# Streaming heads moved around the second layer in a two-layer decode kernel, with double loads for them and two norm stages in one step

## The chip, the cores and the metric

The kernel runs on one core of one Trainium2 chip. The metric is the device time of one execution in microseconds (us); lower is better. The core has a tensor engine (PE; its weight loads are listed apart as PEld), a vector engine (DVE), a scalar engine (ACT), GpSimd (POOL) and SyncE (SP), which here issues nearly all DMA transfers. Sixteen DMA engines move the data from HBM to the on-chip memory (SBUF).

## The reference

Eight sequences decode one token each. A layer is grouped-query attention over a cache, followed by a small dense network, each behind a layer norm and with a residual. Two such layers run one after the other, with the same weights and the same caches:

```python
# x: 8 x 1 x 512; k_cache, v_cache: 8 batches x 8 kv heads x 8192 keys x 128, bf16
# wq: 512 x 4096, wo: 4096 x 512 (32 query heads, 4 to a kv head); w1: 512 x 1792, w2: 1792 x 512
def _A_ref(x, k_cache, v_cache, wq, wo):
    q = (x @ wq) as 32 heads
    k = jnp.repeat(k_cache, rep, axis=1); v = jnp.repeat(v_cache, rep, axis=1)
    scores = jnp.einsum("bhqd,bhkd->bhqk", q, k) * (Dh ** -0.5)
    p = _softmax(scores, axis=-1)
    return jnp.einsum("bhqk,bhkd->bhqd", p, v) as rows @ wo
def _B_ref(x, w1, w2):
    return _silu(x @ w1) @ w2

x = x + _A_ref(_layernorm(x), A_k_cache, A_v_cache, A_wq, A_wo)
x = x + _B_ref(_layernorm(x), B_w1, B_w2)
x = x + _A_ref(_layernorm(x), A_k_cache, A_v_cache, A_wq, A_wo)
x = x + _B_ref(_layernorm(x), B_w1, B_w2)
```

Each cache has 134 MB in all. Both layers read all of it, so what the first layer leaves in SBUF need not be loaded again for the second.

## The kernel before

**Tasks, steps and pieces.** A task is one kv head of one batch in one layer: `(layer, b, g)`. There are 128. A task has four steps, and a step `c` handles one piece of 2,048 keys (K, 0.5 MB) and one piece of V (0.5 MB). For a K piece PE transposes it in two halves into PSUM (`emit_t`, L545), ACT copies the first half back (L554) and DVE the second (L556), and PE makes the scores (`emit_s`, L579). The softmax of a task runs in the steps after it: maximum on DVE (L590, L592) with a POOL reduction over partitions (L594), exponential on ACT (L603) after L599 and L601, sum (L609, L611), transposes of the probabilities (`emit_pt`, L619). V is used six steps (`LAG`) after K (`emit_pv`, L639).

**The arena.** The pieces live in an arena of 28 slots of 0.5 MB. Five of the eight heads of a batch (heads 3 to 7) are *kept*: the transposed K pieces of the first layer, 20 slots, stay until the second layer has used them (one of them is parked in PSUM for a while), and three V pieces of the last head too. The other three heads (0 to 2) are *streaming*: each layer loads them anew.

**The order of tasks.** `make_tasks` writes the order. For each batch `b` it puts the kept heads of the first layer (five tasks), then a block of streaming tasks, then the second layer of the kept heads (five tasks), and then the kept heads of the next batch. The block has five streaming tasks, six for the first and the last batch. They are the second layer of streaming heads of earlier batches (`behind`) and the first layer of streaming heads of later ones (`ahead`). No streaming task stands between the second layer of a batch and the kept heads of the next. Three streaming tasks end the order.

**The loads.** `plan_loads` and `lay_loads` go through all K and V pieces in the order of need, in half steps, and give each the slot that comes free first; `after` is the half step that frees it. A load may be a *double*: two neighbouring pieces of a head, 1 MB in one DMA into two neighbouring slots, with rows of 8 KB. The kernel before allows doubles for kept heads and for the last batch's second layer, where both slots come free at least 8 half steps (`WIDE`) ahead of need. SyncE issues the loads in the order of this list (`issue_until`), each as soon as its slot is free, and all on one queue: a load whose slot is still in use holds those behind it.

**The chain between the layers.** When the last kept head of a batch is done (`last0`, six steps after its K), its row goes on to the second layer through a chain of small jobs: the rest of the output projection, a layer norm, the dense network, another layer norm, and the queries of the second layer. The jobs stand in a list, and each step of the tasks takes at most one of each kind in the step's own order: `MID` in its middle, `TILE` ahead of its scores on PE, `TURN` at its end. A layer norm has four stages: `n[0]` sums on DVE and POOL (L661, L663), `n[1]` centres and sums squares (L669, L689, L690 on DVE, L692 on POOL), `n[2]` reads POOL's sum and makes a first guess at the root (L708, L710, L698, L703), and `n[3]` makes a second and scales the row (L698, L703, L717). The engines take their instructions in the order written, so on DVE the stages stand between the copies L556 and the maximum L590.

Of the kernel before, what the change touches and what calls it, by code (L numbers as in the profile page):

```python
# [17 lines left out]
KEEP = 20  # L18
KEEPV = 3
PARK = 1  # L20
LAG = 6
WIDE = 8
AHEAD = 8
# [114 lines left out]
def make_tasks(nb, nkv, keep_from):  # L138


    first = int(keep_from)
    a = [[(0, b, g) for g in range(first)] for b in range(nb)]
    kept = [[(0, b, g) for g in range(first, nkv)] for b in range(nb)]
    c = [[(1, b, g) for g in range(first, nkv)] for b in range(nb)]
    d = [[(1, b, g) for g in range(first)] for b in range(nb)]
    ahead = [t for b in range(1, nb) for t in a[b]]
    behind = []
    tasks = a[0] + kept[0]
    na = 0
    for b in range(nb):  # L150
        if b:
            tasks += kept[b]
        size = -(-(2 * first * (nb - 1)) // nb) if b in (0, nb - 1) else 2 * first * (nb - 1) // nb
        must = max(0, first * min(b + 1, nb - 1) - na)
        nd = size if b == nb - 1 else min(len(behind), first, size - must)
        tasks += behind[:nd]
        del behind[:nd]
        take = ahead[na:na + size - nd]
        na += len(take)
        tasks += take  # L160
        if b + 1 == nb:
            tasks += behind
        tasks += c[b]
        behind += d[b]
    tasks += d[nb - 1]
    assert na == len(ahead)
    return tasks


def rows_of(d, kept):  # L170
    return 0 if (d.g, d.k) in kept else d.layer, d.b, d.g, d.k // 2
# [22 lines left out]
def lay_loads(tasks, kept, parked, keptv, nslot, ngran, single):  # L194

    at = {t: i for i, t in enumerate(tasks)}
    wanted = []
    late = closing_from(tasks, kept)
    for i, (layer, b, g) in enumerate(tasks):
        for k in range(ngran):  # L200
            c = i * SPT + k
            if layer == 0 or (g, k) not in kept:
                last = i if layer or (g, k) not in kept - parked else at[(1, b, g)]
                wanted.append(Load("K", layer, b, g, k, -1 if c < AHEAD else 2 * (c - LEAD if c >= late else c), 2 * (last * SPT + k) + 1))
            elif (g, k) in parked:
                wanted.append(Load("C", layer, b, g, k, 2 * (c - 1), 2 * c + 1))
            if layer == 0 or (g, k) not in keptv:
                last = i if layer or (g, k) not in keptv else at[(1, b, g)]
                wanted.append(Load("V", layer, b, g, k, 2 * (c + LAG), 2 * (last * SPT + k + LAG)))
    wanted.sort(key=lambda d: (d.need, d.kind))  # L210
    free = [-2] * nslot
    loads, copies = [], []
    while wanted:
        d = wanted.pop(0)
        if d.kind == "C":
            d.slot = max((j for j in range(nslot) if free[j] < d.need - 1), key=lambda j: (free[j], j))
            free[d.slot] = d.free
            copies.append(d)
            continue
        mate = None  # L220
        if d.k % 2 == 0 and ((d.g, d.k) in kept or d.layer and d.b == tasks[-1][1]) and rows_of(d, kept) not in single:
            same = [e for e in wanted if (e.kind, e.layer, e.b, e.g, e.k) == (d.kind, d.layer, d.b, d.g, d.k + 1)]
            mate = same[0] if same else None
            s = min(range(nslot - 1), key=lambda j: (max(free[j], free[j + 1]), j))
            after = max(free[s], free[s + 1])
            if after > d.need - WIDE or d.need < 0 or len(wanted) == 1:
                mate = None
        if mate:
            wanted.remove(mate)
# [27 lines left out]
def _build(ctx, nc, A_x, A_k_cache, A_v_cache, A_wq, A_wo, B_w1, B_w2, out):  # L257
    B, _sq, D = A_x.shape
# [3 lines left out]
    REP = HQ // HKV  # L262
    KT = D // 128
# [168 lines left out]
    with nc.Block() as block:  # L432

        @block.sync
        def _(sync_eng):
# [346 lines left out]
                )  # L782

            TILE, MID, TURN = range(3)

            def chain_of(b):
                x0, x1, x2 = [XT[n][:, :, b:b + 1] for n in range(3)]
                xn = one[2]
                qt2, rq2 = QT2[b % 2], f"QT2_{b % 2}"

                def attended():
                    sum_rows(x1, "XT1", x0, "XT0", 1.0)

                def up():
                    tiles([(t, xn[:, k, :], across(w1_sb[:, k, :], 0, FT)[:, t], k == 0, k == KT - 1)
                           for k in range(KT) for t in range(NT)], ["w1", "xn1"])

                hv = MISC[:, 0:FT * QR:QR]

                def expo():  # L800
                    upright(FT)
                    op(act, lambda: act.activation(eh, hv, ACT.Tanh, scale=0.5), reads=["MISC"], writes=["eh"])

                def silu():
                    op(dve, lambda: dve.scalar_tensor_tensor(hsT, eh, 1.0, hv, op0=ALU.add, op1=ALU.mult),
                       reads=["MISC", "eh"], writes=["hsT"])

                def down(q0, q1):
                    def run():
                        tiles([(t, hsT[:, q:q + 1], across(w2_sb[:, q, :], 0, KT)[:, t], q == 0, q == FT - 1)  # L810
                               for q in range(q0, q1) for t in range(NT)], all_of("w2") + ["hsT"])
                    return run

                AC = KB // QR

                def ask(a, k0, k1):
                    def run():
                        tiles([(t, xn[:, k, :], across(wq_sb[:, k, :], a * AC, (a + 1) * AC)[:, t],
                                k == 0, k == KT - 1) for k in range(k0, k1) for t in range(NT)], ["wq", "xn1"])
                    return run  # L820

                def answer(a):
                    def run():
                        upright(AC)
                        op(dve, lambda: dve.tensor_copy(qt2[:, a * AC:(a + 1) * AC], MISC[:, 0:KB:QR]),
                           reads=["MISC"], writes=[rq2])
                    return run

                n1, n2 = ln_stages(x1, "XT1", 1, one), ln_stages(x2, "XT2", 1, one)

                def gained():
                    sum_rows(x2, "XT2", x1, "XT1", 0.5)
                    n2[0]()

                def met():
                    attended()
                    n1[0]()

                return (
                    [(TURN, met), (MID, n1[1]), (MID, n1[2]), (TURN, n1[3])]  # L840
                    + [(TILE, up), (MID, expo), (TURN, silu), (TILE, down(0, FT // 2)), (TILE, down(FT // 2, FT))]
                    + [(TURN, gained), (MID, n2[1]), (MID, n2[2]), (TURN, n2[3])]
                    + [x for a in range(HQ // AC)
                       for x in ((TILE, ask(a, 0, KT // 2)), (TILE, ask(a, KT // 2, KT)), (TURN, answer(a)))]
                )

            def closing(n):
# [94 lines left out]
            emit_q(0)  # L942

            chain = []
            chain_b = [None]
            turn = [0]
            last0 = {b: max(task_at[(0, b, g)] for g in range(HKV)) for b in range(B)}
            first1 = {b: min(task_at[(1, b, g)] for g in range(HKV)) * SPT for b in range(B)}
# [19 lines left out]
            for c in range(NC + LAG):  # L968
                if c < NC:
                    layer, b, g, k = where(c)  # L970
                if c and c % SPT == 0 and c < NC:
                    assert layer == 0 or not chain or chain_b[0] != b
                    emit_q(c // SPT)
                ready = c < NC and (c < AHEAD or layer == 1 and (g, k) in kept)
                if ready:
# [24 lines left out]
                if c >= LAG and (c - LAG) % SPT == SPT - 1:  # L1000
                    tj = (c - LAG) // SPT
                    layer, b, g = tasks[tj]
                    if layer == 0:
                        heads[b].append(g)
                    elif b == B - 1:
                        heads[B].append(g)
                    if layer == 0 and tj == last0[b]:
                        assert not chain and turn[0] == b
                        chain.extend([(TILE, lambda b=b: add_rest(b))] + chain_of(b))
                        chain_b[0] = b  # L1010
                        turn[0] = b + 1
            assert not queue and not chain

# [38 lines left out]
```

## Time and profile before

| | |
|---|---|
| median of 3 runs | 1145.84 us (1143.29 to 1145.88) |
| the profiled execution | 1136.29 us |
| its span, first to last instruction | 1134.5 us |
| mean granted PE clock | 0.926 of full speed |
| PE busy | 935.0 us, 82% |
| DVE, ACT, POOL busy | 49%, 43%, 10% |
| HBM read | 452.47 MB |
| time of SyncE's queue on the 16 DMA engines | 99.1% of the span |

The page divides the span into 40 slices; the DMA row gives the mean busy share of the 16 DMA engines in tenths, and the row below it the GB/s that they moved. A stretch of time can be asked for by itself; its line gives the stretch, its length, the busy time of PE, PEld, DVE, ACT and POOL with the number of instructions, the granted PE clock, the DMA share and the GB/s. A timeline line gives the start, the length, engine, source line, operation, what is written and read, and in brackets the idle time before it and what ended it.

### The profile page before, as it was taken

The numbers are of one execution on the slowest core, as the hardware profiler recorded it, in microseconds if no ns is written. First come the engines' busy times: TensorE is split into PE (matmuls) and PEld (weight loads), VectorE is DVE, ScalarE is ACT, GpSimd is POOL, SyncE is SP. The second block draws the span as 40 slices with busy tenths as digits, with TensorE's granted clock in tenths as the row PEclk, the third lists the DMA queues.
The fourth block names the chain that finished last, engine by engine and source line by source line (L and its number), as shares of the span: only waits on it lengthen the run. The fifth ranks groups of instructions, "written<-read, shape, count | busy, mean of one in ns | idle before, by whom it ended". The sixth has DMA issues, their size and how long they took to land.

```text
span 1134.5 us, 42794 instructions
## 1 busy us (share of the span) xinstructions
PE 935.0 (82%) x18792; PEld 698.9 (62%) x18792; DVE 558.3 (49%) x1710; ACT 491.0 (43%) x778; POOL 117.3 (10%) x300
## 2 busy tenths in 40 slices
PE   6687887888888888888888888888878888888796
PEld 4366664666566665666567665676566655665565
DVE  6444554445534553446444553446444553455444
ACT  5354442455335542554245542554245432554332
POOL 0000111001100101001100111001100111011010
PEclk9699998999879997999889997999789997999888
DMA  9999999999999999999999999999999999999995
GB/s 376 413 413 415 392 407 412 420 411 385 405 419 416 391 408 417 419 411 392 412 419 415 394 403 418 418 403 393 407 419 411 381 408 419 417 388 367 396 420 224
DMA packets 95550, 455.26 MB, mean 401 GB/s; under 512 B 10620, under 2 KB 10884, under 8 KB 69380
## 3 DMA queue, kind: packets, MB, share of 16 engines
q1 hardware_dynamic: 95348, 452.51, 99.1%
q8 instruction: 148, 2.42, 0.9%
q14 instruction: 38, 0.31, 0.1%
q10 hardware_dynamic: 16, 0.01, 0.0%
HBM read 452.47 MB, written 0.01 MB: 399 GB/s over the span
## 4 chain that ended last, share of the span: by engine, by line
DMA 40%; PE 37%; DVE 11%; ACT 5%; issue 5%; SPq 2%; POOL 0%; POOLq 0%; ACTq 0%; DVEq 0%
DMA arena<-in_A_v_cache_dram 32%; PE TPp L545 18%; PE SCp L579 9%; DVE arena L556 9%; DMA arena<-in_A_k_cache_dram 7%; PE OTp L639 4%; ACT arena L554 4%; PE TPp L619 2%; DMA wq<-in_A_wq_dram 2%; SPq L401 2%; PE MISC L754 2%; ACT P L603 1%; PE KEPTp L545 1%; DVE small L628 1%; DVE small L599 0%
## 5 line engine op out<-in xcount | busy, mean ns | idle before, releaser
L554 ACT COPY arena<-TPp 128x1024 bf16<-128x1024 bf16 x344 | 348.1, 1012 | 393.1 <-PE TPp L545 389.7
L545 PE MATMUL TPp<-ident,arena 128*128 128x128 bf16 x5504 | 377.8, 223 | 28.1 <-DMA arena<-in_A_k_cache_dram 22.3
L556 DVE COPY arena<-TPp 128x1024 bf16<-128x1024 bf16 x344 | 238.0, 692 | 329.7 <-PE TPp L545 327.0
L545 PEld LDWEIGHTS TPp<-ident,arena 128*128 128x128 bf16 x5504 | 317.9, 100 | 118.1 <-issue 62.1
L639 PE MATMUL OTp<-PT,arena 128*128 128x32 bf16 x8192 | 292.0, 179 | 56.6 <-DMA arena<-in_A_v_cache_dram 52.7
L639 PEld LDWEIGHTS OTp<-PT,arena 128*128 128x128 bf16 x8192 | 252.6, 97 | 136.0 <-DMA arena<-in_A_v_cache_dram 105.7
L579 PE MATMUL SCp<-arena,QB 128*32 128x512 bf16 x2048 | 223.8, 429 | 71.5 <-DVE arena L556 24.0
L603 ACT ACTIVATE P<-SCp,small 128x512 bf16<-128x512 f32 x128 | 87.9, 687 | 203.5 <-DVE small L601 157.8
L590 DVE TENSOR_REDUCE small<-SCp 128x1 f32<-128x512 f32 x128 | 88.5, 692 | 103.7 <-PE SCp L579 102.5
L579 PEld LDWEIGHTS SCp<-arena,QB 128*32 128x32 bf16 x2048 | 59.8, 96 | 112.5 <-ACT arena L554 53.4
L594 POOL PARTITION_ALL_REDUCE small<-small x128 | 47.5, 371 | 620.9 <-DVE small L592 620.9
L611 POOL PARTITION_ALL_REDUCE small<-small x128 | 55.2, 431 | 332.4 <-DVE at L653 146.5
L619 PE MATMUL TPp<-ident,P 128*128 128x128 bf16 x512 | 54.9, 235 | 26.4 <-ACT arena L554 14.6
L619 PEld LDWEIGHTS TPp<-ident,P 128*128 128x128 bf16 x512 | 31.5, 103 | 35.5 <-ACT arena L554 20.1
L623 DVE COPY PT<-TPp 128x256 bf16<-128x256 bf16 x128 | 37.3, 291 | 20.8 <-PE TPp L619 18.9
L609 DVE TENSOR_SCALAR small<-small 128x4 f32<-128x4 f32 x128 | 28.7, 224 | 37.9 <-ACT P L603 37.9
L592 DVE TENSOR_SCALAR small<-small 128x4 f32<-128x4 f32 x128 | 29.4, 229 | 4.5
L599 DVE TENSOR_TENSOR small<-small 128x4 f32<-128x4 f32 x128 | 20.0, 157 | 20.9 <-POOL small L594 20.9
L767 DVE STREAM_TRANSPOSE MISC<-MISC 128x128 f32<-128x128 f32 (+2 forms) x40 | 22.1, 552 | 10.0 <-PE MISC L754 10.0
L754 PE MATMUL MISC<-wo,at 128*32 128x128 bf16 x1024 | 26.0, 231 | 0.0
L603 ACT ACTIVATION_READ_ACCUMULATOR P<-SCp,small 128x1 f32 x128 | 24.7, 193 | 0.0
L601 DVE TENSOR_REDUCE small<-small 128x1 f32<-128x4 f32 x128 | 20.1, 157 | 4.4
(102 smaller groups left out, 329.7 us busy)
## 6 DMA issues: line engine op xcount, KB each, us to landing
arena<-in_A_v_cache_dram SPq DMA_DIRECT2D x131, 1024.0 KB, 13.8
arena<-in_A_v_cache_dram SPq DMA_DIRECT2D x226, 512.0 KB, 6.6
arena<-in_A_k_cache_dram SPq DMA_DIRECT2D x216, 512.0 KB, 7.2
arena<-in_A_k_cache_dram SPq DMA_DIRECT2D x68, 1024.0 KB, 20.1
arena<-in_A_wo_dram SPq DMA_DIRECT2D x8, 512.0 KB, 12.7
wq<-in_A_wq_dram SPq DMA_DIRECT2D x1, 4096.0 KB, 24.8
w<-in_B_w_dram SPq DMA_DIRECT2D x1, 1792.0 KB, 22.3
arena<-in_B_w_dram SPq DMA_DIRECT2D x3, 512.0 KB, 16.9
```

Source lines behind the costliest of these rows:

```text
L545: lambda c=c: pe.transpose(tpv[:, c, :], chunk(slot, h * GRP + c), ident[:, :])
L554: op(act, lambda: act.copy(dst, bank[:, :]), reads=[rt], writes=[r_half(slot, h)])
L556: op(dve, lambda: dve.tensor_copy(dst, bank[:, :]), reads=[rt], writes=[r_half(slot, h)])
L579: lambda t=t: pe.matmul(SCp[bank][t * QR:(t + 1) * QR, :], QB[qn][:, NGRAN - 1 - k:NGRAN - 1 - k + QR], keys[:, t * KB:(t + 1) * KB], star ...
L590: op(dve, lambda: dve.tensor_reduce(mxp[st][:, :], SCp[bank][:, :], AX.X, ALU.max), reads=[f"SC{bank}"], writes=[f"mxp{st}"])
L594: op(pool, lambda: pool.partition_all_reduce(mxa[st][:, :], mxr[st][:, :], 128, bass.bass_isa.ReduceOp.max), reads=[f"mxr{st}"], writes=[f ...
L603: op(act, lambda: act.activation(P[:, :], SCp[bank][:, :], ACT.Exp, bias=nb[st][:, 0:1], scale=SM_SCALE, accum_out=rs[st][:, :]), reads=[f ...
L611: op(pool, lambda: pool.partition_all_reduce(ssa[st][:, :], ssm[st][:, :], 128, bass.bass_isa.ReduceOp.add), reads=[f"ssm{st}"], writes=[f ...
L619: lambda c=c: pe.transpose(tpv[:, c, :], P[:, c * 128:(c + 1) * 128], ident[:, :])
L623: op(dve, lambda: dve.tensor_copy(PT[:, :, :, :], tpv.rearrange("p c (t q) -> p c t q", q=QR)[:, :, :, 0:NGRAN * REP]), reads=[f"TP{tb}"], ...
L639: lambda n=n, cc=cc: pe.matmul(otp, chunk(slot, n), PT[:, cc % CPB, (cc // CPB) % NT, cc // (CPB * NT)::NGRAN].unsqueeze(2).to_broadcast([ ...
L754: lambda t=t, col=col, w=w, start=start, stop=stop: pe.matmul(MISC[t * QR:(t + 1) * QR, 0:math.prod(w.shape[1:])], spread(col), w, start=s ...
```

## The change

It makes three edits.

1. `make_tasks` puts four streaming tasks (`WINDOW`) between the kept heads of a batch and its second layer. The remaining ten go behind the second layer, one or two ahead of each batch's next kept heads: 1, 1, 2, 1, 2, 1, 2 behind batches 0 to 6. In both places tasks of `behind` come first, as far as enough of `ahead` is done in time.
2. `lay_loads` allows a double for any pair of pieces; the rule on half steps ahead and the rule that a row of pieces is laid out in one way in all its loads stay.
3. In the chain, stages `n[2]` and `n[3]` of both layer norms become one `TURN` job, at the end of the step whose middle takes `n[1]`. The chain gets two steps shorter. The assertion ahead of a second-layer task no longer wants the whole chain done, but the queries of that head (`asked`); it costs no instruction.

```diff
+WINDOW = 4
...
+    rest = 2 * len(ahead) - nb * WINDOW
+
+    def put(size, must):
+        nonlocal na, tasks
+        nd = max(0, min(len(behind), size - max(0, must - na)))
+        tasks += behind[:nd]
+        del behind[:nd]
+        tasks += ahead[na:na + size - nd]
+        na += len(ahead[na:na + size - nd])
+
     for b in range(nb):
         if b:
             tasks += kept[b]
-        size = -(-(2 * first * (nb - 1)) // nb) if b in (0, nb - 1) else 2 * first * (nb - 1) // nb
-        must = max(0, first * min(b + 1, nb - 1) - na)
-        nd = size if b == nb - 1 else min(len(behind), first, size - must)
-        tasks += behind[:nd]
-        del behind[:nd]
-        take = ahead[na:na + size - nd]
-        na += len(take)
-        tasks += take
-        if b + 1 == nb:
-            tasks += behind
+        gap = rest * (b + 1) // (nb - 1) - rest * b // (nb - 1) if b + 1 < nb else 0
+        due = first * min(b + 1, nb - 1)
+        put(WINDOW if b + 1 < nb else len(behind), due - gap)
         tasks += c[b]
         behind += d[b]
-    tasks += d[nb - 1]
+        if b + 1 < nb:
+            put(gap, due)
+    tasks += behind
...
-        if d.k % 2 == 0 and ((d.g, d.k) in kept or d.layer and d.b == tasks[-1][1]) and rows_of(d, kept) not in single:
+        if d.k % 2 == 0 and rows_of(d, kept) not in single:
...
-                    [(TURN, met), (MID, n1[1]), (MID, n1[2]), (TURN, n1[3])]
+                    [(TURN, met), (MID, n1[1]), (TURN, row(n1[2], n1[3]))]
...
-                    + [(TURN, gained), (MID, n2[1]), (MID, n2[2]), (TURN, n2[3])]
+                    + [(TURN, gained), (MID, n2[1]), (TURN, row(n2[2], n2[3]))]
                     + [x for a in range(HQ // AC)
-                       for x in ((TILE, ask(a, 0, KT // 2)), (TILE, ask(a, KT // 2, KT)), (TURN, answer(a)))]
+                       for x in ((TILE, ask(a, 0, KT // 2)), (TILE, ask(a, KT // 2, KT)), (TURN, answered(a)))]
...
-                    assert layer == 0 or not chain or chain_b[0] != b
+                    assert layer == 0 or asked[b] >= (g + 1) * REP
```

`row(f, g)` runs its parts one after the other; `answered` is `answer` with a note of how many heads have their queries.

More of the change, by code (lines that the diff above doesn't have):

```diff
@@ L784, in _ @@
             TILE, MID, TURN = range(3)
+            asked = [0] * B
             def chain_of(b):
@@ L837, in met, with row, run, answered @@
                     n1[0]()
+                def row(*parts):
+                    def run():
+                        for f in parts:
+                            f()
+                    return run
+                def answered(a):
+                    def run():
+                        answer(a)()
+                        asked[b] = (a + 1) * AC
+                    return run
                 return (
-                    [(TURN, met), (MID, n1[1]), (MID, n1[2]), (TURN, n1[3])]
+                    [(TURN, met), (MID, n1[1]), (TURN, row(n1[2], n1[3]))]
                     + [(TILE, up), (MID, expo), (TURN, silu), (TILE, down(0, FT // 2)), (TILE, down(FT // 2, FT))]
-                    + [(TURN, gained), (MID, n2[1]), (MID, n2[2]), (TURN, n2[3])]
+                    + [(TURN, gained), (MID, n2[1]), (TURN, row(n2[2], n2[3]))]
                     + [x for a in range(HQ // AC)
-                       for x in ((TILE, ask(a, 0, KT // 2)), (TILE, ask(a, KT // 2, KT)), (TURN, answer(a)))]
+                       for x in ((TILE, ask(a, 0, KT // 2)), (TILE, ask(a, KT // 2, KT)), (TURN, answered(a)))]
                 )
@@ L944, in _ @@
             chain = []
-            chain_b = [None]
             turn = [0]
@@ L1009, in _ @@
                         chain.extend([(TILE, lambda b=b: add_rest(b))] + chain_of(b))
-                        chain_b[0] = b
                         turn[0] = b + 1
```

## The prediction

> **What bounds the kernel now.** I read the page first (engines, slices, DMA issues), then busy time by stretches, then the timeline of one step. The page:
>
> ```profile
> PE 935.0 (82%) x18792; PEld 698.9 (62%) x18792; DVE 558.3 (49%) x1710; ACT 491.0 (43%) x778; POOL 117.3 (10%) x300
> DMA  9999999999999999999999999999999999999995
> GB/s 376 413 413 415 392 407 412 420 411 385 405 419 416 391 408 417 419 411 392 412 419 415 394 403 418 418 403 393 407 419 411 381 408 419 417 388 367 396 420 224
> ...
> q1 hardware_dynamic: 95348, 452.51, 99.1%
> ...
> arena<-in_A_v_cache_dram SPq DMA_DIRECT2D x131, 1024.0 KB, 13.8
> arena<-in_A_v_cache_dram SPq DMA_DIRECT2D x226, 512.0 KB, 6.6
> arena<-in_A_k_cache_dram SPq DMA_DIRECT2D x216, 512.0 KB, 7.2
> arena<-in_A_k_cache_dram SPq DMA_DIRECT2D x68, 1024.0 KB, 20.1
> ```
>
> The transfers fill 99.1% of the span, so the kernel is bound by its 452.5 MB and only the rate can change: 420 GB/s at best, with a dip once per batch. One rotation (heads kept for batch 1, then the streaming block, then the second layer) by stretches; the last two columns are DMA share and GB/s:
>
> ```profile
> 171.80:202.80 31.00, 23.38 (x472) 14.70 (x468) 12.45 (x46) 7.14 (x19) 4.37 (x11) 0.81 1.01 412
> 202.80:249.70 46.90, 40.01 (x832) 32.63 (x820) 22.20 (x59) 23.84 (x33) 4.00 (x10) 0.98 1.02 417
> 249.70:268.20 18.50, 15.68 (x332) 12.87 (x332) 10.12 (x32) 9.85 (x14) 2.40 (x6) 1.00 1.00 376
> 268.20:297.80 29.60, 25.68 (x520) 18.51 (x520) 17.57 (x58) 13.95 (x21) 2.84 (x7) 1.00 1.02 405
> 297.80:328.20 30.40, 25.19 (x476) 15.71 (x468) 12.27 (x46) 6.88 (x18) 4.37 (x11) 0.71 1.01 412
> ```
>
> These are second-layer kept heads, first-layer kept heads, the first two streaming tasks, the other three, and second-layer kept heads again. The dip, 376, is in the first two streaming tasks. The trace says why. There the plan frees slots slowly (the arena goes from 25 usable slots to 6): SyncE issues at 257.16, 259.43 and 261.82 us, one load per 2.3 us, where a load of 0.5 MB needs 1.29 us at 408 GB/s. The pieces in flight, 8 at 242 us, drain to 4 at 264 us, and at 4 the rate is down. Steps meanwhile run at 2.27 us, the pace of PE itself (about 9.2 us a task); afterwards the tasks take 10.2 to 11 us, DMA's pace.
>
> **Part 1, double loads.** The built program issues 225 doubles and 390 singles where the page counts 199 and 442. All ten tasks behind the second layer come in doubles; kept heads lose 18 doubles to alignment. So 52 singles become 26 doubles, 27.3 MB. Singles alone ran at 407 GB/s (408:420 us), doubles at 419 (204:216 us): 27,260/407 − 27,260/419 = 67.0 − 65.1 = 1.9 us less. Bounds: 0 (a double must wait for the later of two slots, and a wait at the queue's head holds all behind it) and 2.7 less (packets of 4 KB at about 163 ns in pairs against 314 ns, 3,328 pairs over 16 engines, plus their completions). I take −1.9. All bytes stay, and every task keeps its instructions on PE, DVE, ACT and POOL.
>
> The Trainium skill's "DMA: Bandwidth & Descriptors", section "Measured", lists one transfer of 64 KB at 0.95 us and of 1 MB at 6.15 us and advises at least 1 MiB each; by a straight line through them (an estimate) one double would save 0.6 us over two singles, 26 of them 16 us in place of the 1.9 above. This trace disagrees as it stands: queued singles keep 407 GB/s.
>
> **Part 2, four tasks before the second layer, ten behind.** Against 408 GB/s the eight streaming blocks run at 400, 394, 398, 398, 396, 393, 391 and 377, so each loses length × (1 − rate/408): 1.2, 1.7, 1.2, 1.2, 1.4, 1.8, 2.0 and 4.7 us. The first and last:
>
> ```profile
> 112.90:171.80 58.90, 50.18 (x996) 37.42 (x996) 32.17 (x100) 28.73 (x42) 6.05 (x15) 1.00 1.02 400
> 1002.90:1064.50 61.60, 50.52 (x996) 37.88 (x996) 32.24 (x100) 28.72 (x42) 6.05 (x15) 0.97 0.99 377
> ```
>
> In the first block DMA had been late already (V pieces landed with no lead, kept tasks took 9.8 us), so its queue was fuller; its 1.2 us is what a block costs anyway. What the others lose above it is 0.5, 0, 0, 0.2, 0.6, 0.8 and 3.5, together 5.6 us. How much does a streaming task ahead of the kept heads win back? Count pieces. From 202.8 to 268.2 us, 65.4 us, seven tasks use 53 pieces; at 415 GB/s DMA could land 51.8. With 4 pieces landed and unused at the start, 2.8 would be left, but the slots allow 1 (six ahead, five of them in flight): 1.8 pieces of DMA time are lost, 2.3 us, against 1.7 read off. One more task uses 8 pieces in at least 9.2 us, in which DMA lands 7.3: surplus 1.1. Two more: 0.4. So a gap of one task (before the kept heads of batches 1, 2, 4, 6) wins 40% and a gap of two (3, 5, 7) nearly 80%. Batches 1, 2, 4, 6: 0.4 × 1.5 = 0.6. Batches 3 and 5: 0.8 × 0.6 = 0.5. In batch 7 a single step of 5.60 us (up projection waiting for a late K) makes most of the 3.5, and may not recur; I count 0.6 of it, 2.1. Sum −3.2. The ten moved tasks also leave the tight slots, where the first block loses 0.2 us a task, mostly in the steps that stay: −0.5. Bounds for this part: 0 and −7.5 (5.6 + 1.9). I take −3.7.
>
> The order of issue into the tight block is the same in both plans (5, 7, 6, then 8 pieces a task), so the dip cannot vanish by itself; only a fuller queue covers it. The first second-layer task now lets 4 pieces issue in most batches where it was 6; batch 3 of before had 4 and its stretch ran at the same rate as the others, so nothing is charged. The second layer finds its queries in time: the chain starts ten steps before it, the first half of the queries is answered in the ninth, the second half at the first second-layer step, three steps before use.
>
> **Part 3, both root stages at one step's end.** This is the new wait. Before, the stage that reads POOL's sum runs a step later, when the sum is long there:
>
> ```profile
> 1018.21 0.69 DVE L556 COPY arena<-TPp 128x1024 bf16<-128x1024 bf16 x1 [0.57 <-PE TPp L545]
> ...
> 1019.20 0.16 DVE L690 TENSOR_REDUCE small<-small 128x1 f32<-128x4 f32 x1
> 1019.49 0.69 DVE L590 TENSOR_REDUCE small<-SCp 128x1 f32<-128x512 f32 x1
> 1020.22 0.23 DVE L592 TENSOR_SCALAR small<-small 128x4 f32<-128x4 f32 x1
> 1020.48 0.69 DVE L556 COPY arena<-TPp 128x1024 bf16<-128x1024 bf16 x1
> ...
> 1021.35 0.14 DVE L708 TENSOR_SCALAR small<-small 128x1 f32<-128x1 f32 x1
> ...
> 1022.61 0.16 DVE L717 TENSOR_TENSOR tiny<-small 128x4 bf16<-128x4 f32 x1
> 1019.45 0.40 POOL L692 PARTITION_ALL_REDUCE small<-small  x1 [1.33 <-DVE small L690]
> ```
>
> Now L708 to L717 stand right behind L690, ahead of L590. POOL ends at 1019.85; with the 0.17 us that L599 needs after L594, L708 starts at 1020.02, the row of seven takes 1.42 us (1021.35 to 1022.77), L590 and L592 0.99, and the eviction L556 starts at 1022.43 instead of 1020.48: 1.95 us late. Queued behind it are the scores on PE, and behind those the K slot that SyncE waits for. Before, the up projection one step later waited for the same root (steps of 3.2 to 3.4 us, 0.9 over 2.27); it now falls into that stall, so 1.0 us net. The second norm's root comes at a step without L590: 0.66 for POOL plus 1.42, less the 1.1 us by which the eviction is later anyway: 1.0. So 2.0 us of PE's path per batch, 16 in all. It is covered by DMA: five pieces in flight are 6.4 us of transfers, and tight steps have 2.57 − 2.27 = 0.3 us of slack each. The up steps of before, 0.9 long, stand in the first block that lost 1.2 us in all, so most is hidden; but the first stall falls where the queue is shortest. I charge 0.25 us per batch, +2.0. Bounds: 0 and +16.
>
> **Sum.** −1.9 − 3.7 + 2.0 = −3.6 us: the profiled execution (1136.29 us, span 1134.5) would become 1132.7. The median of the runs, 1145.84, is 0.8% above the profiled one, which changes the difference by 0.03: 1142.2.
>
> **Rivals.**
> - *The cover holds* (faster, 1136): the stalls cost nothing and all 5.6 us of dips go, −1.9 − 7.5 = −9.4, 1136.4. For it: DMA share of 1.00 and more in nearly all stretches. Against: the dip's issue order is unchanged.
> - *Each load has a fixed cost* (faster, 1138.9): a single lands in 6.6 us with five in flight, 5 × 1.29 = 6.4, which leaves 0.2 per load; 26 fewer loads bring 5.2 in place of 1.9, −6.9. Against: loads overlap. The skill's rule above is its kin.
> - *The dips stay* (same, 1144): slots, not the queue, decide, the stalls hide, and only the doubles count: −1.9.
> - *The root stall reaches DMA* (slower, 1155): at the first stall only 4 pieces are in flight, already too few for the full rate. If DMA idles through each stall, +16 − 1.9 − 3.7 = +10.4, 1156; with 0.9 of it passed on, about 1155. It decides from the point where DMA's share in the stretch around the first stall falls below 0.9, as in 1020:1032 us of before (0.90, 336 GB/s, a 5.60 us step).
>
> **How the numbers follow.** A measurement of this kernel tells about 0.3%, 3.4 us, from no change. My sum is −3.6, on that edge: I give it 0.45, and split it 0.25 faster and 0.20 same. The cover holds 0.18, fixed cost 0.05, dips stay 0.14, stall reaches DMA 0.18. Faster 0.48, same 0.34, slower 0.18. Range 1134 to 1154: down to the fully covered case with 2 us of the runs' own spread (1143.29 to 1145.88), up to the stall passed on for the most part, leaving out about 0.1 on each side.
>
> **What would show it.** Right: 225 doubles and 390 singles; streaming blocks at 396 or more GB/s, the last above 385; an eviction about 2 us late behind a root, with the first norm's POOL sum named as its waiter; DMA share near 1.00 around it. Wrong: stretches under 340 GB/s right at the roots (stall not covered), or gaps and kept heads under 410 GB/s (doubles blocking the queue's head), or blocks no better than 394 on average.

## The result and the profile after

The changed kernel took 1136.29 us (median of 13 runs, 1132.43 to 1142.22) beside 1143.29 us for the kernel before in the same comparison (13 runs, 1136.62 to 1146.5). The ratio is 0.9949, interval 0.9924 to 0.9974: 5.8 us faster (3.0 to 8.7), where 3.6 were forecast. (The ratio is not that of the two medians, which differ by 7.0.) The forecast median was 1142.2; of the 5.9 us by which the measured one is lower, 2.6 are the kernel before, at 1143.29 here and 1145.84 in its first three runs. A second comparison of the same two kernels gave 0.9956 (0.9933 to 0.998), so the gain is real but about half a per cent.

The profiles alone would have said the opposite. The profiled execution of the changed kernel took 1142.22 us (span 1140.4), the longest of its 13 runs; that of the kernel before took 1136.29, below all 13 of its runs in the comparison. The page of the changed kernel:

```profile
PE 932.1 (82%) x18792; PEld 702.9 (62%) x18792; DVE 555.1 (49%) x1710; ACT 491.8 (43%) x778; POOL 117.3 (10%) x300
DMA  9999999999999999999999999999999999999995
GB/s 375 416 415 414 377 384 419 418 400 395 415 419 412 378 418 418 418 410 390 415 419 410 393 407 418 418 410 381 385 418 412 388 360 411 418 414 371 391 418 218
...
q1 hardware_dynamic: 91604, 452.51, 98.7%
...
arena<-in_A_v_cache_dram SPq DMA_DIRECT2D x141, 1024.0 KB, 19.3
arena<-in_A_v_cache_dram SPq DMA_DIRECT2D x206, 512.0 KB, 7.0
arena<-in_A_k_cache_dram SPq DMA_DIRECT2D x184, 512.0 KB, 9.5
arena<-in_A_k_cache_dram SPq DMA_DIRECT2D x84, 1024.0 KB, 22.1
```

The loads are the 225 doubles (141 + 84) and 390 singles (206 + 184) that were forecast, for the same 452.51 MB, and the transfers still fill 98.7% of the span. So the kernel is bound as before, and the time is again decided by the dips in the row of GB/s. By stretches, three of the eight streaming blocks of four tasks (the second, the fifth and the last), and then two tasks behind the second layer; the columns are length, PE, PEld, DVE, ACT, POOL, granted clock, DMA share and GB/s:

```profile
240.10:279.50 39.40, 34.34 (x696) 25.47 (x700) 22.04 (x75) 18.87 (x28) 4.43 (x11) 1.00 1.00 392
625.80:665.70 39.90, 34.60 (x700) 25.56 (x700) 22.03 (x75) 18.87 (x28) 4.44 (x11) 1.00 1.02 397
1028.70:1070.10 41.40, 34.89 (x696) 26.33 (x700) 22.17 (x75) 18.87 (x28) 4.43 (x11) 0.96 0.98 372
...
434.60:453.00 18.40, 15.32 (x315) 12.55 (x314) 8.87 (x24) 9.07 (x12) 1.60 (x4) 1.00 1.01 419
```

The tasks that moved behind the second layer run at 417 to 420 GB/s, free of the dip. The four that stayed hold the tight slots and nothing else, and run at 370 to 397. What the merged root does is seen in the timeline of VectorE and GpSimd around the first norm in the second block (start, duration, engine, line):

```profile
256.43 0.69 DVE L562 COPY arena<-TPp 128x1024 bf16<-128x1024 bf16 x1 [0.47 <-PE TPp L551]
...
257.42 0.16 DVE L696 TENSOR_REDUCE small<-small 128x1 f32<-128x4 f32 x1
258.10 0.15 DVE L714 TENSOR_SCALAR small<-small 128x1 f32<-128x1 f32 x1 [0.52 <-POOL small L698]
...
259.38 0.16 DVE L723 TENSOR_TENSOR tiny<-small 128x4 bf16<-128x4 f32 x1
259.46 0.68 DVE L596 TENSOR_REDUCE small<-SCp 128x1 f32<-128x512 f32 x1
...
260.31 0.69 DVE L562 COPY arena<-TPp 128x1024 bf16<-128x1024 bf16 x1
...
257.67 0.40 POOL L698 PARTITION_ALL_REDUCE small<-small  x1 [1.22 <-DVE small L696]
```

VectorE waits 0.52 us for GpSimd's sum, works the root from 258.10 to 259.54, and only then reaches the softmax maximum and its eviction. Evictions of VectorE stand 3.88 us apart (256.43 to 260.31) where the pace is 2.27: 1.6 us late. The same 3.87 to 3.88 stands in every block.

### The profile page after: what moved, and what is told of

It is laid out like the page before. It is cut to its first block, busy times and chain, and to the rows that moved or that the text cites. A ratio compares the mean times of both kernels' runs of the same rounds, so it can differ in the third digit from the quotient of the medians.

```text
span 1140.4 us, 42713 instructions
## 1 busy us (share of the span) xinstructions
PE 932.1 (82%) x18792; PEld 702.9 (62%) x18792; DVE 555.1 (49%) x1710; ACT 491.8 (43%) x778; POOL 117.3 (10%) x300
## 3 DMA queue, kind: packets, MB, share of 16 engines
q1 hardware_dynamic: 91604, 452.51, 98.7%
## 4 chain that ended last, share of the span: by engine, by line
DMA 46%; PE 33%; DVE 11%; ACT 4%; issue 4%; SPq 2%; POOL 0%; POOLq 0%; ACTq 0%; DVEq 0%
DMA arena<-in_A_v_cache_dram 28%; DMA arena<-in_A_k_cache_dram 16%; PE TPp L551 16%; PE SCp L585 8%; DVE arena L562 7%; PE OTp L645 4%; ACT arena L560 4%; DMA wq<-in_A_wq_dram 2%; SPq L407 2%; PE MISC L760 2%; PE TPp L625 2%; DVE small L596 1%; PE KEPTp L551 1%; ACT P L609 1%; DVE small L605 0%
## 5 line engine op out<-in xcount | busy, mean ns | idle before, releaser
L551 PE MATMUL TPp<-ident,arena 128*128 128x128 bf16 x5504 | 383.0, 225 | 25.5 <-DMA arena<-in_A_k_cache_dram 20.2
L551 PEld LDWEIGHTS TPp<-ident,arena 128*128 128x128 bf16 x5504 | 322.2, 100 | 110.9 <-issue 67.5
L585 PE MATMUL SCp<-arena,QB 128*32 128x512 bf16 x2048 | 218.6, 416 | 71.8 <-DVE arena L562 26.9
L625 PE MATMUL TPp<-ident,P 128*128 128x128 bf16 x512 | 54.1, 233 | 31.6 <-ACT arena L560 18.4
```

What stands on the lines that cost most here:

```text
L551: lambda c=c: pe.transpose(tpv[:, c, :], chunk(slot, h * GRP + c), ident[:, :])
L585: lambda t=t: pe.matmul(SCp[bank][t * QR:(t + 1) * QR, :], QB[qn][:, NGRAN - 1 - k:NGRAN - 1 - k + QR], keys[:, t * KB:(t + 1) * KB], star ...
L625: lambda c=c: pe.transpose(tpv[:, c, :], P[:, c * 128:(c + 1) * 128], ident[:, :])
```

## The experiments

All ratios are to the kernel before, on the same chip, with 95% intervals. Where a stretch's **loss** is given, it is the stretch's length less what its packets need at full rate (163 ns for 4 KB, 314 ns for 8 KB, 16 engines), summed over the streaming blocks between kept heads and second layer (42 tasks in before's order, 32 in the new) and worked out from the trace. It is 8.7 us in the profiled execution of before. It is a number of one execution: two profiles of the same work as before (the second with one more memset) give 8.7 and 10.3, two of the changed kernel 14.5 and 10.3, so a difference of 2 to 4 us between two kernels says little by itself.

**The changed kernel again.** No edit.

> The changed kernel as it is, once more, for a second profile beside the first. The profiled execution of the changed kernel took 1142.2 us, the longest of its thirteen runs, and showed streaming blocks at 375 to 397 GB/s. Theory (fuller queue, stalls mostly hidden): a more usual execution of 1132 to 1138 us has blocks at 390 GB/s or more, with the step behind the first root still near 3.9 us. Rival (the stall of the root reaches DMA in every run): blocks stay near 384 GB/s on average whatever the time, and the kernel gains elsewhere. Ratio to before: 0.995 in both.

1137.4 us, 0.9956 (0.9933 to 0.998); the profiled execution took 1135.07. Against the first profile of the same kernel (1142.22) this is 7 us less: the loss in the blocks is 10.3 us here and 14.5 there, and in the second layer's kept heads behind them −0.1 and 3.1. The last section says what else differed.

**The doubles alone**, with before's order and chain:

```diff
-        if d.k % 2 == 0 and ((d.g, d.k) in kept or d.layer and d.b == tasks[-1][1]) and rows_of(d, kept) not in single:
+        if d.k % 2 == 0 and rows_of(d, kept) not in single:
```

> The order and chain of before, with doubles allowed for every pair. In that order it yields 179 doubles instead of 199 (14 for streaming heads, 165 for kept ones), since alignment costs kept heads more than streaming heads win. Theory (doubles are worth the rate difference of 407 to 419 GB/s): 20 fewer doubles are 40 more singles, 21 MB, 1.5 us slower, ratio 1.001. Rival (each load has a fixed cost of 0.2 us): 20 more loads, 4 us slower, ratio 1.0035. Rival (a double needs two free slots and blocks the queue's head): fewer doubles make it faster by 1 us or more.

1135.79 us, 0.9946 (0.9918 to 0.9974), faster, where my theory had 1.5 us slower. In the old order the rule gives fewer doubles, not more: 179, since head 6 of the kept heads loses 24 of its 45. That fits the last rival, that a double blocks the queue's head, and points to head 6, not to the rate of doubles: 5.99 pieces are in flight in the first two streaming tasks, where before has 5.32 (the mean over batches two to eight, counted from issues and landings). This one line by itself gave as much as the whole change: on the same chip its median is 1.6 us below the changed kernel's (3.6 lower to 2.3 higher).

**The merged roots alone**, with before's order and loads:

```diff
-                    [(TURN, met), (MID, n1[1]), (MID, n1[2]), (TURN, n1[3])]
+                    [(TURN, met), (MID, n1[1]), (TURN, row(n1[2], n1[3]))]
...
-                    + [(TURN, gained), (MID, n2[1]), (MID, n2[2]), (TURN, n2[3])]
+                    + [(TURN, gained), (MID, n2[1]), (TURN, row(n2[2], n2[3]))]
```

> The order and loads of before, with the two root stages as one job at the step's end. Theory: eight first-norm steps of about 3.9 us instead of 2.27 and the up step behind them back at 2.3 to 2.4, mostly hidden by transfers: 1 to 3 us slower, ratio 1.001 to 1.003. Rival (the stall reaches DMA): 8 us or more slower, ratio above 1.007, and streaming blocks under 390 GB/s. Rival (no cost at all, the up step's wait only moves): ratio 1.000.

1149.23 us, 1.0058 (1.0028 to 1.0089): slower by 6.6 us (3.2 to 10.2). The step behind the first root is 3.88 us in every block, and the loss in the blocks is 13.6 us beside before's 8.7. So 4.9 of the 5.35 us by which this profiled execution is the longer (1141.64 beside 1136.29) stand in the blocks, where the roots do; against the other profile of before's work the loss is 3.3 us higher. The execution is one of the fastest of its kernel (1140.98 to 1154.85), so it shows less than the 6.6.

**The order and the merged roots, with before's rule for doubles** (187 of them): the first diff reversed in the changed kernel.

> The new order and the merged roots, with the rule for doubles of before: 187 doubles where the changed kernel has 225; all streaming tasks behind the second layer come in singles. Theory (rates 407 and 419): 38 fewer doubles cost 40 MB x (1/407 - 1/419) = 2.8 us against the changed kernel, so the ratio to before is 0.9975, and the stretches behind the second layer fall from 419 to 408 GB/s. Rival (all of the gain is the order): ratio as the changed kernel, 0.995. Rival (all of it is the doubles): ratio 1.000 or above.

1139.48 us, 0.9964 (0.9934 to 0.9993). On the same chip it is 9.7 us below the merged roots alone (resampling both sets of runs gives 4.6 to 12.9): this is the order, with one thing that came along: the old rule gives 187 doubles in the new order, and all 12 that are missing are head 6's. The changed kernel on that chip was 2.1 us lower still (4.4 lower to 0.6 higher): these are the doubles.

**Before with one more memset of the identity**, to see what a rebuilt program of the same work does.

> The kernel before with one more clearing of the identity tile on POOL at the start, where POOL is idle; plan, order and chain are untouched. It asks whether the 0.54% that the doubles rule alone brought in the order of before, with 20 fewer doubles, can be a matter of the run or of the program's place and not of the doubles. Theory (the rule on doubles has a real effect of its own): ratio 1.000, within 0.2%. Rival (any rebuilt program lies 0.3 to 0.6% from before): ratio at 0.997 or under, or at 1.003 or above.

1140.45 us, 1.0005 (0.9983 to 1.0026): nothing.

**Before with singles only** (840 of them): the test that drops a second piece made always true.

```diff
-            if after > d.need - WIDE or d.need < 0 or len(wanted) == 1:
+            if True:
                 mate = None
```

> The order and chain of before, and no doubles at all: 840 single loads, each piece contiguous in memory. Theory of the prediction (rate difference of 407 to 419 GB/s): 209 MB at the lower rate, 209,000 x (1/407 - 1/419) = 14.7 us slower, ratio 1.013, and all stretches at 405 to 410 GB/s. Rival (a double holds the queue's head until two neighbouring slots are free, and fewer doubles keep more transfers in flight): less than 5 us slower, or faster. Rival (each load costs 0.2 us by itself): 199 more loads, 40 us slower, ratio 1.035.

1145.83 us, 1.0048 (1.0031 to 1.0065). The rates of 407 and 419 GB/s ask for 14.7 us more; 5.5 came. Part of what was won back is in the queue: the loss in the blocks fell to 6.2 us from 8.7, and in the first two streaming tasks 6.26 pieces are in flight, where before has 5.32. Where the rest of the 9.2 us was won is not shown.

**Before without doubles in head 6** (154 doubles):

```diff
-        if d.k % 2 == 0 and ((d.g, d.k) in kept or d.layer and d.b == tasks[-1][1]) and rows_of(d, kept) not in single:
+        if d.k % 2 == 0 and d.g != 6 and ((d.g, d.k) in kept or d.layer and d.b == tasks[-1][1]) and rows_of(d, kept) not in single:
```

> The kernel before, except that head 6, the fourth kept head, never takes doubles (154 in all instead of 199). In the order of before the new rule on doubles took them from half of this head and gave almost nothing to streaming heads, and that version was 0.54% faster; at the start of its streaming blocks one piece more was in flight in most batches (7 and 6 against 6 and 5). Theory (a double late in the kept stretch waits for two slots and lets the queue run thin where the slots get few; singles keep it fuller): faster than before by 0.3 to 0.6%, ratio 0.994 to 0.997. Rival (head 6 is not the place; only chance or the four streaming doubles did it): 45 fewer doubles cost 47 MB x (1/407 - 1/419) = 3.3 us, ratio 1.003. Rival (nothing but the rates cancel): 0.999 to 1.001.

1137.54 us, 0.9973 (0.995 to 0.9995). Fewer doubles in that head alone make the kernel faster; the interval holds most of what was expected and the middle falls just short. It is half of what the doubles rule alone brought, although head 6 loses 45 doubles here and 24 there: head 6 matters, but that it is the whole of that gain is not shown. The queue is again fuller, 6.12 pieces. The rate in the first two streaming tasks of the seventh and eighth batches, before first:

```profile
877.30:895.70 18.40, 15.64 (x329) 12.77 (x329) 10.02 (x31) 9.85 (x14) 2.40 (x6) 1.00 0.99 367
1002.90:1021.30 18.40, 15.48 (x328) 12.77 (x329) 10.02 (x31) 9.85 (x14) 2.40 (x6) 1.00 1.01 375
```

Without doubles in head 6:

```profile
880.90:900.50 19.60, 16.70 (x328) 12.68 (x329) 10.04 (x31) 9.86 (x14) 2.40 (x6) 1.00 1.01 394
1007.20:1027.00 19.80, 16.94 (x332) 12.72 (x332) 10.10 (x32) 9.85 (x14) 2.40 (x6) 1.00 1.01 395
```

The two tasks take longer (PE goes at DMA's pace), but DMA moves 394 and 395 GB/s in place of 367 and 375. Over batches two to eight the mean is 391 beside 383; one batch, the fourth, went the other way (374 beside 395). A double waits for two adjacent slots at the head of SyncE's queue; head 6 is the last but one ahead of the block.

**The first norm's root as a job of its own behind the next step's eviction**, in the changed kernel, with the up projection one step later:

```diff
-                    [(TURN, met), (MID, n1[1]), (TURN, row(n1[2], n1[3]))]
+                    [(TURN, met), (MID, n1[1]), (MID, row(n1[2], n1[3])), (TURN, lambda: None)]
```

> The changed kernel with the first norm's root as one job in the middle of the step after, behind that step's eviction, and the up projection one step later still; the second norm's root stays at its step's end. The chain is one step longer and still answers the first half of the queries ahead of the second layer. Theory (the root stall reaches DMA, 6.6 us for both norms in the order of before): the 3.88 us step goes back to 2.3 to 2.4 us in every block, and the kernel gains 3 to 5 us on the changed one, ratio to before 0.991 to 0.993. Rival (in the new order the stall is covered): no gain, ratio 0.995 to 0.996, although the step is short again.

1138.01 us, 0.9987 (0.9965 to 1.0008), a miss: no gain over the changed kernel, but some 3.9 us more (0.7 to 7.1, both intervals taken together). The 3.88 us step is gone (2.36 to 2.48), but the step with the up projection is now 3.4 us, and half of the queries' work slides into the second layer's first steps, whose kept stretch loses 5.2 us beside −0.1 in the changed kernel's second profile.

**The changed kernel without the root**: the third stage is skipped for the chain's two norms, and the fourth scales by whatever stands in its tile. VectorE's seven instructions and the wait for GpSimd's sum fall to one instruction.

> The changed kernel, with the root work of the sixteen chain norms left out: DVE neither reads POOL's second sum nor computes the root, it only scales the row by whatever stands in the root's place. This is the price of both stalls together in the new order. Theory (stalls reach DMA): both steps fall to 2.3 to 2.8 us and the kernel gains 5 to 8 us on the changed one, ratio to before 0.988 to 0.991. Rival (as predicted, mostly covered): it gains 2 us or less, ratio 0.993 to 0.996.

1129.51 us, 0.9909 (0.9877 to 0.994), so 5.0 us below the changed kernel (0.9953, the mean of its two ratios); with both intervals, 0.9 to 9.1. Five of the six runs lie within 1 us (1128.79 to 1129.6). The loss in the blocks is 5.4 us beside 10.3 in the changed kernel's second profile.

**ScalarE copies both halves in the step behind a merged root**, in the changed kernel; the root and its wait stay.

```diff
-                if h == 0:
+                if h == 0 or rooted[0]:
+                    rooted[0] = rooted[0] and h == 0
                     op(act, lambda: act.copy(dst, bank[:, :]), reads=[rt], writes=[r_half(slot, h)])
...
                             f()
+                        rooted[0] = True
                     return run
```

> The changed kernel, but in the step behind each merged root ACT copies both halves of the keys back, so the scores no longer wait for DVE's root; nothing is left out. Theory (the root holds PE through the eviction, and that costs 5 us as leaving the root out showed): the step behind the first root falls from 3.88 to 3.2 us or less and the one behind the second from 3.2 to 2.8, the kernel gains 2 to 5 us on the changed one, ratio to before 0.990 to 0.993. Rival (ACT's second copy of 1.01 us, ahead of the exponential, only replaces the stall): ratio 0.995 to 0.997 and steps of 3.5 us or more.

1131.11 us, 0.9924 (0.9897 to 0.9951): the lowest median of the versions that compute everything. It is faster than the kernel before; by ratio it is 3.3 us below the changed kernel, but with both intervals 0.4 above to 6.9 below, so it can't be told from it by itself. The loss in the blocks is 8.2 us beside 10.3. The same place in its timeline:

```profile
255.73 0.15 DVE L716 TENSOR_SCALAR small<-small 128x1 f32<-128x1 f32 x1 [0.53 <-POOL small L700]
...
257.08 0.68 DVE L598 TENSOR_REDUCE small<-SCp 128x1 f32<-128x512 f32 x1
...
255.88 1.93 ACT L562 COPY arena<-TPp 128x1024 bf16<-128x1024 bf16 x2 [1.16 <-PE TPp L552]
```

While VectorE is in the root, ScalarE copies both halves in 1.93 us and is done at 257.81. In the changed kernel VectorE's half came 1.85 us (260.31 less 258.46) behind the start of ScalarE's and was done at 261.00, 2.54 us after it. The step is 3.17 us in place of 3.88, the next 2.92 in place of 2.38: the delay of the softmax maximum stays. The two steps together are 6.09 us in place of 6.26, so most of the stall moves on by a step; without the root they are 5.3 to 5.9.

**The same with the softmax maximum ahead of the root:**

```diff
-                step(TURN)
                 soft(c - SPT + 1, softmax_max)
+                step(TURN)
```

> As the kernel in which ACT copies both halves behind a root, and the maximum of the scores goes ahead of the root on DVE, while POOL still sums; the exponential then is not late by the root's 1.4 us. Theory (after the eviction the next to wait is the exponential and the transposes of the probabilities behind it): a further 1 to 2 us, ratio to before 0.989 to 0.992. Rival (up projection then waits for the root that is now later by 0.4 us): equal to the version without, within 0.1%.

1133.77 us, 0.9918 (0.9889 to 0.9947): not to be told from the version before it.

**The merged roots alone, with both halves on ScalarE** (before's order and loads, the two edits shown above together).

> The order and loads of before with the merged roots, and ACT copying both halves in the step behind each root. Merged alone that order was 0.58% slower than before; the same remedy brought the changed kernel from about 0.995 to 0.992. Theory (the price of the merge is the wait of the scores for DVE's root, in either order): the ratio to before falls from 1.006 to 1.000 to 1.003. Rival (the merge costs through something else, such as the up projection running a step earlier in the thinnest part of the queue): 1.005 or more, as without the remedy.

1142.22 us, 1.0018 (0.9988 to 1.0048). Of the merged roots' 0.58% about 0.4% goes with the eviction, 4.6 us with an interval of −0.3 to 9.5; the rest can't be told from nothing. The loss in the blocks is 11.2 us, between the 8.7 and 10.3 of before's work and the 13.6 with VectorE's half behind the root.

## Why the prediction was right, and where its terms were not

The sign held, and −3.6 lies inside the measured interval (−3.0 to −8.7). That the size came so near is luck: two terms were too small, with opposite signs, and their errors of −6.0 and +4.6 us mostly cancel. Nor does the number choose between the rivals: "each load has a fixed cost" named −6.9, inside the interval too, and "the cover holds" named 1136.4, nearly the measured median, but as −9.4 from a higher start, and its condition, stalls that cost nothing, failed. The terms:

| term | forecast | measured | from |
|---|---|---|---|
| doubles | −1.9 (0 to −2.7) | −2.1 (−4.4 to +0.6) | changed kernel less order with merge |
| order | −3.7 (0 to −7.5) | −9.7 (−12.9 to −4.6), with 12 doubles fewer in head 6 | order with merge less merge alone |
| merged roots | +2.0 (0 to +16) | +6.6 (+3.2 to +10.2) | merge alone |
| sum | −3.6 | −5.2 | the steps lead from before to the changed kernel on one chip, so this is their difference there (0.9956) and no separate test of the parts |

**Merged roots.** The mechanism was as forecast: the wait named, the eviction 1.6 us late beside 1.95 forecast, the row of seven 1.44 us (258.10 to 259.54) beside 1.42. The stall of the first norm was a little smaller than charged: its two steps take 6.26 us (3.88 + 2.38), where before took 5.5 to 5.7 (2.27 + 3.2 to 3.4) in most blocks, 0.6 to 0.8 net in place of 1.0. What failed is the step from the engine's time to the kernel's: 0.25 us of the 2.0 us per batch was charged as passed on, and about 0.8 (6.6 / 8) was. That is the rival "the root stall reaches DMA" in kind, at 40% where that rival took 90%. Two kinds of experiment point to the eviction as a carrier: leaving the root out wins 5.0 us, and leaving it where it is but giving the eviction to ScalarE takes 0.4% of 0.58% away. The second is not clear of noise by itself, and moving the first norm's root behind the eviction won nothing, since the up projection and the queries then came late: that a root at the step's end costs time is shown, how much of it goes through the eviction is not settled. The reason that I had given for the cover, that the up steps of before are late too and sit in a block that loses little, did not bear: the blocks' loss rose from 8.7 (10.3 in the other profile of the same work) to 13.6 us. DMA's share did not show it: it reads 0.98 to 1.02 in blocks of 370 to 397 GB/s.

**Order.** The mechanism holds in kind: with the order, merged roots and before's doubles 5.68 pieces are in flight in the first two streaming tasks, with merged roots alone 5.38, in before 5.32 (5.90 and 5.89 in the two profiles of the changed kernel), and the ten moved tasks run at 417 to 420 GB/s. The size failed: −3.7 lies outside the interval, the lower end of the bounds, −7.5, inside it. One part that the term left out is head 6. The forecast took the 18 doubles that the kept heads lose as a price; all 18 are head 6's, and 12 of them go with the order alone. In the old order fewer doubles in that head made the kernel faster (0.9946 with 24 fewer, 0.9973 with 45) and the queue fuller (5.99 and 6.12 pieces), so part of the −9.7 can be theirs; no run has the new order with head 6's doubles kept. Another part was that I measured the dips in one profiled execution, 1136.29 us, which is at the fast end of its kernel's runs: it showed less to win than a usual one. The profile of the same work with one more memset took 1139.41 us, and its first two streaming tasks in those two batches run at

```profile
882.20:900.60 18.40, 15.47 (x329) 12.78 (x330) 10.02 (x31) 9.85 (x14) 2.41 (x6) 1.00 0.99 359
1009.10:1027.50 18.40, 15.48 (x328) 12.77 (x328) 10.01 (x31) 9.85 (x14) 2.41 (x6) 1.00 0.98 364
```

beside 367 and 375; over batches two to eight 374.4 beside 382.9 in the mean, 2.9 us (7 × 18.4 × 8.5/383) of the 3.1 between the two executions. Whether this is all of the missing 6 us stays open: no profiled execution of the kernel before fell among its longer ones, and the profile of the order with before's doubles (1142.04, of runs from 1133.79 to 1144.93) was a long one of its own kernel. Nor was the order tried without merged roots; the pair with ScalarE's copies, which has the order and the doubles between them, gives 0.9924 / 1.0018 = 0.9906, of the same size.

**Doubles.** In the new order the term stands within its interval. But the working behind it, that a double is worth its packets' rate and no more, was incomplete: in the old order the same rule won 0.54% with 20 doubles fewer, at least in part by head 6's loss of them, and giving up every double cost 5.5 us where the rate says 14.7. A double also empties the queue ahead of a place with few slots: without head 6's doubles 6.12 pieces are in flight there, with them 5.32. The rival "each load has a fixed cost" falls with it: 199 loads more would have cost 40 us by its 0.2 us each, beside 5.5. The Trainium skill's "DMA: Bandwidth & Descriptors", section "Measured", advises at least 1 MiB to a transfer, from a table of transfers issued from GpSimd; by the straight line that the prediction drew through that table, giving up 199 doubles would cost 119 us (an estimate, 199 × 0.6). The run, with loads issued from SyncE, measured 5.5, and the measurement decides.

**The signs that were named.** The loads and the gaps (417 to 420 against 410) came as said. "Blocks at 396 or more, the last above 385" did not: 370 to 397, and 371 to 395 in the second profile. The sign of being wrong, "blocks no better than 394 on average", came instead: 384 in the first profile and 389 in the second, where before has 393. It was the wrong mark: the forecast took the rate of blocks of five and six tasks, which hold easy tasks too, over to blocks of the four tight ones. By that sign the kernel should have gained nothing; the times say otherwise. The sign "under 340 GB/s right at the roots" came in one of the sixteen steps with a first root (303, in the second profile).

## What to carry to other kernels

In a kernel that loads fill, look at the number of pieces in flight where slots are fewest, not at the mean rate: what empties the queue there (a double that waits for two slots, a late eviction) can cost more than a faster transfer brings. All fourteen profiles together, cut into stretches of 4 us from 60 to 1085 us, show by how much: with 4 pieces in flight (rounded) the mean rate is 370 GB/s, with 5 it is 392, with 6 it is 405, with 10 or more 412 to 421. A wait that is put ahead of an eviction on a vector engine is a wait of TensorE and of the slots behind it; another engine that has room may take that one copy. And where a change has parts, run them singly: here −10 and +7 us hid in −6, one line of it did as much alone in the old order, and one profile of each kernel pointed the wrong way.

## What the runs showed that was not expected

TensorE's granted clock falls to one half inside busy blocks. In the first profile of the changed kernel it did so in four streaming blocks (at 146.2, 794.8, 924.5 and 1040.5 us), each time for 3.4 us, in the second profile in none; in that of before once, at 1024.2 us, inside the 5.60 us step that the prediction read as a late K alone (TensorE's wait for that K is 1.47 us). The first one, in TensorE's timeline and then in stretches of 1 us:

```profile
143.88 1.07 PE L551 MATMUL TPp<-ident,arena 128*128 128x128 bf16 x16
146.16 0.60 PE L645 MATMUL OTp<-PT,arena 128*128 128x32 bf16 x16 [1.22 <-DMA arena<-in_A_v_cache_dram]
```

```profile
145.00:146.00 1.00, 0.00 (x0) 0.00 (x0) 0.86 (x6) 0.55 (x1) 0.00 (x0) 1.00 1.02 418
146.00:147.00 1.00, 0.83 (x20) 0.76 (x20) 0.97 (x4) 0.00 (x0) 0.10 (x1) 0.62 1.04 418
147.00:148.00 1.00, 1.00 (x14) 0.29 (x12) 0.29 (x1) 0.00 (x0) 0.33 (x1) 0.50 1.03 422
...
150.00:151.00 1.00, 1.00 (x31) 0.56 (x27) 0.78 (x2) 0.61 (x1) 0.00 (x0) 1.00 0.99 311
```

TensorE waits 1.22 us for a V piece while VectorE is in the second norm's root; the clock stands at 0.50 for the next 3.4 us, its matmuls take 1.5 to 1.7 times as long, and its slots come free later: from 150 to 154 us DMA moves 274 to 340 GB/s, where it had moved 356 to 422 in the eight before. In the 4 us from the second step behind this root on, it moves 315 here, and 411 in the second profile, which has no spell there. The Trainium skill's "TensorE: Matmul & The Clock Gate", Part 1, "What's actually happening", has such windows of about 3.4 us that run freely, with half or full speed and nothing between; the records agree. But the page asks for a whole idle window, and here none was: in the 3.41 us ahead of this spell, 142.8 to 146.2 us, TensorE's matmuls were busy for 53%. The streaming blocks of all fourteen profiles hold ten such spells, and each follows 3.41 us with 43 to 58% busy; three stretches of 51 to 57%, counted on the same grid of 3.41 us, were not followed by one, and none that was busier was.

That these spells are the 7 us between the two profiles is likely by their places. The four blocks with a spell, with the second-layer kept heads behind them, lose 9.2 us more in the first profile than in the second, the other four 1.6 us less. No run changes the spells alone.
